# Moving the second gate pass and dealing layer 2 out in even pieces in a Fourier-mixing and gated feed-forward kernel

## Chip, cores, metric

One core of one Trainium2 chip. The time is device microseconds of one execution. The kernel before takes 719.3 us (median of 4 runs, 718.97 to 719.59); repeated runs agree within about 0.15%. One execution of the kernel before was a slow one (1024.69 us at a clock of 0.662); it is left out.

## The reference

```python
def _attn_ref(x):                       # x: 8 x 3008 x 256
    X = np.fft.fft(x, axis=1)
    X = np.fft.fft(X, axis=2)
    return X.real.astype(np.float32)

def _moe_ref(x, w_gate, w_val, w_out):  # 24064 x 256; 256 x 1536, 256 x 1536, 1536 x 256
    g = x @ w_gate
    gelu = 0.5 * g * (1.0 + erf(g * inv_sqrt2))
    val = x @ w_val
    return (gelu * val @ w_out).astype(np.float32)
```

## The kernel before

The real part of a Fourier transform has a symmetry, so each token is worked out together with its mirror token. E and O are the sum and the difference part of a pair. A gate is computed as E + O; then a third matmul adds -2 O into the same PSUM bank (weights M), and the bank holds the mirror token's gate. The gate's bank is therefore read by a GELU twice, the second time after the third matmul.

There are 8 batches; each has three groups of at most 512 token pairs. A group is worked in 12 *blocks* of 128 hidden columns (`fc`); the stretch of the emitted order that belongs to one block is a *slot*. Two blocks of three are *split* (none in the very first group): the value is taken with two matmuls in two banks, and VectorE (three operations) and GpSimd do the rest. The third kind is unsplit: value matmuls E and O, then M later, each followed by one product on VectorE. Layer 2 of a group (96 matmuls) is dealt out over the 12 slots of the next group, and the transform of the next batch is dealt out as *filler*. An *eviction* is an instruction that copies a full PSUM bank to SBUF, and so lets the bank be used again.

All eight PSUM banks are taken: two for gates, three for values, one for layer 2 outputs, two for the transform.

```python
def ps_g():   return psum_pool.tile([128, 512], FP32, tag="g",   bufs=2, name="ps_g")
def ps_v():   return psum_pool.tile([128, 512], FP32, tag="v",   bufs=3, name="ps_v")
def ps_o():   return psum_pool.tile([128, 2, C], FP32, tag="o",  bufs=1, name="ps_o")
def ps_dft(): return psum_pool.tile([128, 512], FP32, tag="dft", bufs=2, name="ps_dft")

def l1_first(ci, fc):
    def run():
        # ... cut: slices, tiles
        pg = ps_g()
        mm(pg, n, "g", "E", fs, E, True, False)
        mm(pg, n, "g", "O", fs, O, False, True)
        gl = gelu_tile()
        nc.scalar.activation(gl[:, 0, :n], pg[:, :n], AF.Gelu)              # L517, first GELU
        pv = ps_v()
        if apart(ci, fc):                                                   # split block
            mm(pv, n, "v", "E", fs, E, True, True)
            po = ps_v()
            mm(po, n, "v", "M", fs, O, True, True)
            # ... ve on VectorE from pv (L524), two halves of vv from po (L528, L530)
        else:
            mm(pv, n, "v", "E", fs, E, True, False)
            mm(pv, n, "v", "O", fs, O, False, True)
            # ... first product on VectorE (L536)
    return run

def l1_second(ci, fc):
    def run():
        # ... cut
        mm(pg, n, "g", "M", fs, O, False, True, skip_group_check=True)      # second gate pass
        if apart(ci, fc):
            # ... second GELU (L550), product on GpSimd (L551)
        else:
            mm(pv, n, "v", "M", fs, O, False, True, skip_group_check=True)
            # ... second GELU (L554), second product on VectorE (L555)
    return run

def l2_unit(ci, sub, sign):       # 12 matmuls of 256 columns into one half of the ps_o bank
    ...

def s1_pack(j0):                  # transform, first stage: 8 matmuls, two evictions on ScalarE (L379)
    def run():
        s1_mm(j0)
        s1_ev(j0, "AA")
    return run

# the loop over the blocks of a group
            for fc in range(NFC):
                first[fc]()
                # ... early work and weight folds of the first batch
                tgt = max(0, len(filler) * (slot + 1 - first_slot) // (nslot - first_slot))
                while fi < tgt:
                    filler[fi]()
                    fi += 1
                if fc > 0:
                    second[fc - 1]()
                tgt = len(pend) * (fc + 1) // NFC
                while done < tgt:             # 8 units on 12 slots: 12 matmuls, or none
                    pend[done]()
                    done += 1
                slot += 1
            second[NFC - 1]()
```

The order in which this code emits instructions is not the order on the engines. A scheduler takes it as a priority and moves instructions when, by its own model, an earlier one would wait.

Of the kernel before, what the change touches and what calls it, by code (L numbers as in the profile page):

```python
# [11 lines left out]
AF = mybir.ActivationFunctionType  # L12
# [6 lines left out]
def _sub(base: bass.AP, free_pattern, free_offset, part_start=0, part_num=None):  # L19
    p_step, p_count = base.ap[0]  # L20
    if part_num is None:
        part_num = p_count - part_start
    pat = [[p_step, part_num]] + [list(x) for x in free_pattern]
    off = base.offset + part_start * p_step + free_offset
    return ap_replace(base, ap=pat, offset=off)
# [10 lines left out]
def kernel(  # L36
# [8 lines left out]
    nc = tc.nc  # L45
# [8 lines left out]
    NFC = F // 128  # L54
# [8 lines left out]
    chunk_off, chunk_len = [], []  # L63
    o = 0
    for gr in groups:
        n = sum(width(k2) for k2 in gr)
# [12 lines left out]
    TOK = max(chunk_len)  # L79
# [5 lines left out]
    G = const_pool.tile([NP, NJ, K2H * 4], BF16)  # L85
# [41 lines left out]
    def ps_v():  # L127
        return psum_pool.tile([128, 512], FP32, tag="v", bufs=3, name="ps_v")
# [362 lines left out]
    def ffn_work(b):  # L491
        l1, l2 = [], []
        cstate = {}




        def apart(ci, fc):
            return fc % 3 != 2 and (b, ci) != (0, 0)

        def mm(ps, n, nm, part, fs, src, start, stop, **kw):
            nc.tensor.matmul(ps[:, :n], W[nm, part][:, fs], src, start=start, stop=stop, **kw)  # L502

        def l1_first(ci, fc):
            def run():
                n = chunk_len[ci]
                c0 = chunk_off[ci]
                E, O = (EO_bufs[b][:, i, c0 : c0 + n] for i in range(2))
                if ci not in cstate:
                    cstate[ci] = {"h": h_tile(), "ps": {}, "pso": {}}  # L510
                st = cstate[ci]
                fs = slice(fc * 128, (fc + 1) * 128)
                pg = ps_g()
                mm(pg, n, "g", "E", fs, E, True, False)
                mm(pg, n, "g", "O", fs, O, False, True)
                gl = gelu_tile()
                nc.scalar.activation(gl[:, 0, :n], pg[:, :n], AF.Gelu)  # L517
                pv = ps_v()
                if apart(ci, fc):
                    mm(pv, n, "v", "E", fs, E, True, True)  # L520
                    po = ps_v()
                    mm(po, n, "v", "M", fs, O, True, True)
                    ve = ve_tile()
                    nc.vector.scalar_tensor_tensor(  # L524
                        ve[:, :n], EB_bufs[b][:, c0 : c0 + n], w128[:, fc : fc + 1], pv[:, :n],
                        op0=ALU.mult, op1=ALU.add)
                    vv = v_tile()
                    nc.vector.scalar_tensor_tensor(  # L528
                        vv[:, 0, :n], po[:, :n], -0.5, ve[:, :n], op0=ALU.mult, op1=ALU.add)
                    nc.vector.scalar_tensor_tensor(  # L530
                        _sub(vv, [[-1, n]], TOK + n - 1), po[:, :n], 0.5, ve[:, :n], op0=ALU.mult, op1=ALU.add)
                    st["ps"][fc] = (pg, vv, gl)
                else:
                    mm(pv, n, "v", "E", fs, E, True, False)
                    mm(pv, n, "v", "O", fs, O, False, True)
                    nc.vector.tensor_tensor(st["h"][:, fc, 0, :n], gl[:, 0, :n], pv[:, :n], op=ALU.mult)  # L536
                    st["ps"][fc] = (pg, pv, gl)
            return run

        def l1_second(ci, fc):  # L540
            def run():
                n = chunk_len[ci]
                c0 = chunk_off[ci]
                O = EO_bufs[b][:, 1, c0 : c0 + n]
                st = cstate[ci]
                fs = slice(fc * 128, (fc + 1) * 128)
                pg, pv, gl = st["ps"].pop(fc)
                mm(pg, n, "g", "M", fs, O, False, True, skip_group_check=True)
                if apart(ci, fc):
                    nc.scalar.activation(_sub(gl, [[-1, n]], TOK + n - 1), pg[:, :n], AF.Gelu)  # L550
                    nc.gpsimd.tensor_tensor(st["h"][:, fc, :, :n], gl[:, :, :n], pv[:, :, :n], op=ALU.mult)  # L551
                else:
                    mm(pv, n, "v", "M", fs, O, False, True, skip_group_check=True)
                    nc.scalar.activation(gl[:, 1, :n], pg[:, :n], AF.Gelu)  # L554
                    nc.vector.tensor_tensor(  # L555
                        _sub(st["h"], [[-1, n]], (fc * 2 + 1) * TOK + n - 1),
                        gl[:, 1, :n], pv[:, :n], op=ALU.mult)
            return run

        def last(ci):  # L560
            return b == B - 1 and ci == len(groups) - 1

        def l2_unit(ci, sub, sign):
            def run():
                st = cstate[ci]
                n = chunk_len[ci]
                m = min(128, n - sub * 128)
                h0 = n - sub * 128 - m if sign else sub * 128
                if sign == 0:
                    st["pso"][sub] = ps_o()  # L570
                pso = st["pso"][sub]
                for fc in range(NFC):
                    nc.tensor.matmul(  # L573
                        pso[:m, sign, :],
                        st["h"][:, fc, sign, h0 : h0 + m],
                        Wo_sb[:, fc, :],
                        start=(fc == 0),
                        stop=(fc == NFC - 1),
                    )
                if last(ci):  # L580

                    osb = osb_tile()
                    if sign == 0:
                        nc.vector.tensor_copy(osb[:m, 0, :], pso[:m, 0, :])  # L584
                        store(b, ci, sub, 0, osb[:, 0, :], nc.sync)
                    else:
                        nc.scalar.activation(osb[:m, 1, :], pso[:m, 1, :], AF.Copy)
                        store(b, ci, sub, 1, osb[:, 1, :], nc.scalar)
                elif sign == 1:
                    osb = osb_tile()  # L590
                    nc.scalar.activation(osb[:m], pso[:m], AF.Copy)  # L591
                    store(b, ci, sub, 0, osb[:, 0, :], nc.sync)
                    store(b, ci, sub, 1, osb[:, 1, :], nc.sync)
            return run

        chunks = []
        for ci in range(len(groups)):
            nsub = (chunk_len[ci] + 127) // 128
            first = [l1_first(ci, fc) for fc in range(NFC)]
            second = [l1_second(ci, fc) for fc in range(NFC)]  # L600

            subs = [nsub - 1, *range(nsub - 1)] if last(ci) else range(nsub)
            l2s = [l2_unit(ci, s, g) for s in subs for g in range(2)]
            chunks.append((first, second, l2s))
        return chunks


    head, s1_mm, s1_ev = dft_work(0)
    NHEAD = 5 + 3
    x_tiles.append(x_tile())  # L610
# [52 lines left out]
    pend = []  # L663
    for b in range(B):
        if b + 1 < B:
            if b > 0:
                x_tiles.append(x_tile())
                load_x(b + 1, [(0, 16), (16, 16)])
            filler = dft_work(b + 1)
        else:  # L670
            filler = []
        chunks = ffn_work(b)
        nslot = len(chunks) * NFC
        first_slot = 0
        if b == 0:

            first_slot = NFC
        slot = 0
        fi = 0
        for first, second, l2s in chunks:  # L680
            done = 0
            for fc in range(NFC):
                first[fc]()
                if b == 0 and slot < NFC:
                    for _ in range(2):
                        if early:
                            early.pop(0)()
                    for f in folds.get(slot, []):
                        f()
                tgt = max(0, len(filler) * (slot + 1 - first_slot) // (nslot - first_slot))  # L690
                while fi < tgt:
                    filler[fi]()
                    fi += 1
                if fc > 0:
                    second[fc - 1]()
                tgt = len(pend) * (fc + 1) // NFC
                while done < tgt:
                    pend[done]()
                    done += 1
                slot += 1  # L700
            second[NFC - 1]()
            pend = l2s
    for u in pend:
        u()


# [1 line left out]
_INS = ['x', 'moe_w_gate', 'moe_w_val', 'moe_w_out']  # L708
# [26 lines left out]
```

## Time and profile before

In tables and profile lines, PE is TensorE (PEld its weight loads), DVE is VectorE, ACT is ScalarE, POOL is GpSimd, and L517 is line 517 of the kernel.

| | before |
|---|---|
| time | 719.3 us |
| span of the profiled run | 716.7 us |
| PE / DVE / ACT / POOL busy | 96 / 80 / 65 / 58% |
| all matmuls at the closest spacing seen | 661 us |
| excess over that spacing, whole span | 46 us |
| the same between 45 and 660 us, single gaps under 25 ns left out | 20.6 us |

From the page (engine: busy us, share of the span, instructions), and the chain that ended last:

```profile
PE 688.0 (96%) x5274; PEld 460.5 (64%) x5336; DVE 572.3 (80%) x923; ACT 466.9 (65%) x892; POOL 412.2 (58%) x242
...
PE 88%; ACT 5%; DVE 4%; issue 2%; DMA 1%; POOL 0%; ACTq 0%; DVEq 0%
```

PE's busy time is not a measure of how full it is, because each matmul's record holds its latency too, and records overlap. The Trainium skill comes to the same conclusion ("Perfetto Trace Analysis", section "Identifying the Most-Contended Engine": occupancy of the matmul row is not a good measure of the distance from the roofline, because pipelined instructions look smaller in the trace). In this trace a 512-column matmul has a record of 0.38 us, and the next one starts 0.216 us after it. The *starts* matter: between two starts of 512-column matmuls lie 216 ns in the median, of 481-column ones 204, of 256-column ones 109, of 96-column ones 42. All four are columns/2.4 + 2.5 ns to within about 1 ns, the formula that "TensorE: Matmul & The Clock Gate", section "Back-to-back issue gap", gives for isolated matmuls. So I call *excess* what a start-to-start distance has beyond that; a missing matmul record is filled in by its weight load. Excess is what the rest of this document counts, by the kind of matmul that came late, leaving out single gaps under 25 ns (so counted, the whole span has 44.6 us of it).

| before, 45 to 660 us | excess |
|---|---|
| before the first gate pass | 10.3 us |
| before a value pass | 7.0 us |
| before a transform matmul | 2.8 us |
| before a second gate pass | 0.5 us |
| before a layer 2 matmul | 0.0 us |

The view of waits, for the weight loads (line, ended by: us in total, times, longest). "Issue" means that the profile names no releaser. A weight load starts when the matmul before it has started (WgE at 306.55 below, the next load at 306.56), so idle time before a weight load tells that this matmul came late:

```profile
PEld L502 <- issue: 19.2, 85, 0.4
...
PEld L573 <- issue: 9.4, 26, 0.7
```

The timeline at one such place, ScalarE and then PE with one weight load (start us, us, engine, line, out<-in, count):

```profile
304.60 0.59 ACT L517 ACTIVATE gelu_sb<-ps_g 128x512 bf16<-128x512 f32 x1
305.14 0.87 ACT L379 ACTIVATE A_sb<-ps_dft 128x384 bf16<-128x384 f32 x2
305.90 0.60 ACT L554 ACTIVATE gelu_sb<-ps_g 128x512 bf16<-128x512 f32 x1
306.38 0.62 ACT L550 ACTIVATE gelu_sb<-ps_g 128x512 bf16<-128x512 f32 x1
```

```profile
305.11 0.38 PE L502 MATMUL ps_g<-EO_sb,WgM 128*128 128x512 bf16 x1
305.33 0.38 PE L502 MATMUL ps_v<-EO_sb,WvM 128*128 128x512 bf16 x1
305.56 0.38 PE L502 MATMUL ps_v<-EO_sb,WvE 128*128 128x512 bf16 x1
305.77 0.38 PE L502 MATMUL ps_g<-EO_sb,WgM 128*128 128x512 bf16 x1
305.99 0.49 PE L573 MATMUL ps_o<-Wo_sb,h_sb 128*97 128x256 bf16 x3
306.55 0.38 PE L502 MATMUL ps_g<-EO_sb,WgE 128*128 128x512 bf16 x1
306.56 0.10 PEld L502 LDWEIGHTS <-WgO 128*128 128x128 bf16 x1 [0.25 <-issue]
```

Read it so. The second gate pass (WgM) at 305.11 is followed, in the emitted order, by no layer 2 matmul in this slot, so the next gate pass (WgE) would come at once and want its bank. The scheduler has pulled a value pass, the next second gate pass and three layer 2 matmuls ahead. Still, the bank's GELU (L554) starts at 305.90 and ends at 306.50; WgE starts at 306.55. The third layer 2 matmul started at 305.99 + 2 x 0.109 = 306.21, so WgE could have started at 306.32: 0.23 us lost. This is how the late ones look throughout: between 60 and 660 us, all 66 first gate passes that came over 60 ns late, and whose record is there, start 49 to 51 ns after the end of a GELU.

### The profile page before, as it was taken

Reading aid. Unit: us, or ns where it says so; the run is one execution under the profiler, and the core shown is the slowest. Engines: PE = TensorE matmul, PEld = TensorE weight load, DVE = VectorE, ACT = ScalarE, POOL = GpSimd, SP = SyncE. Lnnn points to the kernel's source line nnn. Section 1 sums busy time; section 2 is a strip of 40 time slices with the busy share of each in tenths; the row PEclk is TensorE's granted clock in tenths of the full one; section 3 lists DMA queues with packets and bytes.
Section 4 is the critical chain, followed back from the end, with each engine's and each line's share of the span. In section 5 each row is a group of like instructions: output and inputs, shape, how many; then the busy total and the mean of one; then the engine's idle time right before and its main releaser. Section 6 shows DMA issues by size and latency. Waiting matters only on the chain.

```text
span 716.7 us, 14298 instructions
## 1 busy us (share of the span) xinstructions
PE 688.0 (96%) x5274; PEld 460.5 (64%) x5336; DVE 572.3 (80%) x923; ACT 466.9 (65%) x892; POOL 412.2 (58%) x242
## 2 busy tenths in 40 slices
PE   2899999999999999999999999999999999999995
PEld 2556666666667666666666666666666766666664
DVE  7698888798877888788877888779887788888870
ACT  6688567766676666766677656776668666666650
POOL 8205565655556565666566656555565656576760
PEclk9999999999999999999999999999999999999999
DMA  9951512431115111151212421111111111211122
GB/s 247 205 118 23 124 31 46 86 72 35 41 38 119 42 34 43 33 121 38 45 31 53 105 45 34 43 36 37 35 41 42 30 44 31 45 41 38 42 45 66
DMA packets 36277, 43.43 MB, mean 61 GB/s; under 512 B 6668, under 2 KB 33292, under 8 KB 34700
## 3 DMA queue, kind: packets, MB, share of 16 engines
q1 hardware_dynamic: 32432, 30.47, 17.8%
q0 software_dynamic: 3184, 11.57, 8.8%
q8 instruction: 41, 0.67, 0.4%
q10 hardware_dynamic: 592, 0.49, 0.3%
q14 instruction: 28, 0.23, 0.1%
HBM read 29.43 MB, written 24.64 MB: 75 GB/s over the span
## 4 chain that ended last, share of the span: by engine, by line
PE 88%; ACT 5%; DVE 4%; issue 2%; DMA 1%; POOL 0%; ACTq 0%; DVEq 0%
PE ps_o L573 33%; PE ps_g L502 23%; PE ps_v L502 20%; PE ps_dft L402 6%; PE ps_dft L365 3%; ACT gelu_sb L517 1%; ACT gelu_sb L554 1%; ACT A_sb L379 1%; PE ps_dft L427 1%; PE ps_dft L440 1%; DVE x_sb L236 1%; ACT out_sb L591 1%; DVE EO_sb L456 1%; PE ps_dft L452 1%; DVE h_sb L536 1%
## 5 line engine op out<-in xcount | busy, mean ns | idle before, releaser
L551 POOL TENSOR_TENSOR h_sb<-gelu_sb,v_sb 128x1024 bf16<-128x1024 bf16 (+1 forms) x184 | 387.1, 2105 | 277.2 <-ACT gelu_sb L550 156.8
L573 PE MATMUL ps_o<-Wo_sb,h_sb 128*128 128x256 bf16 (+1 forms) x2304 | 295.5, 272 | 4.0 <-DVE out_sb L584 2.2
L573 PEld LDWEIGHTS <-h_sb 128*128 128x128 bf16 (+1 forms) x2304 | 227.7, 100 | 68.3 <-issue 9.4
L517 ACT ACTIVATE gelu_sb<-ps_g 128x512 bf16<-128x512 f32 (+1 forms) x288 | 169.8, 590 | 123.2 <-PE ps_g L502 115.2
L524 DVE SCALAR_TENSOR_TENSOR ve_sb<-EB_sb,w_97,ps_v 128x512 f32<-128x512 bf16 (+1 forms) x184 | 134.1, 733 | 66.2 <-PE ps_v L502 66.0
L528 DVE SCALAR_TENSOR_TENSOR v_sb<-ps_v,ve_sb 128x512 f32<-128x512 f32 (+1 forms) x184 | 124.4, 676 | 13.9 <-POOL h_sb L551 0.5
L530 DVE SCALAR_TENSOR_TENSOR v_sb<-ps_v,ve_sb 128x512 f32<-128x512 f32 (+1 forms) x184 | 123.3, 670 | 0.0
L550 ACT ACTIVATE gelu_sb<-ps_g 128x512 bf16<-128x512 f32 (+1 forms) x184 | 108.6, 590 | 19.2 <-PE ps_g L502 17.7
L502 PE MATMUL ps_v<-EO_sb,WvE 128*128 128x512 bf16 (+1 forms) x288 | 107.8, 374 | 3.2
L502 PE MATMUL ps_g<-EO_sb,WgE 128*128 128x512 bf16 (+1 forms) x287 | 107.4, 374 | 1.6
L502 PE MATMUL ps_v<-EO_sb,WvM 128*128 128x512 bf16 (+1 forms) x288 | 108.0, 375 | 0.3 <-DVE v_sb L530 0.2
L502 PE MATMUL ps_g<-EO_sb,WgM 128*128 128x512 bf16 (+1 forms) x287 | 107.9, 376 | 0.1
L555 DVE TENSOR_TENSOR h_sb<-gelu_sb,ps_v 128x512 bf16<-128x512 bf16 (+1 forms) x104 | 69.7, 671 | 32.5 <-ACT gelu_sb L554 32.5
L591 ACT ACTIVATE out_sb<-ps_o 128x512 f32<-128x512 f32 x92 | 54.8, 595 | 51.2 <-PE ps_o L573 51.2
L502 PE MATMUL ps_g<-EO_sb,WgO 128*128 128x512 bf16 (+1 forms) x231 | 86.4, 374 | 0.0
L536 DVE TENSOR_TENSOR h_sb<-gelu_sb,ps_v 128x512 bf16<-128x512 bf16 (+1 forms) x104 | 69.9, 673 | 5.2 <-ACT gelu_sb L517 4.0
L554 ACT ACTIVATE gelu_sb<-ps_g 128x512 bf16<-128x512 f32 (+1 forms) x104 | 61.0, 590 | 6.3 <-PE ps_g L502 6.2
L412 DVE CAST Z_sb<-ps_dft 128x512 bf16<-128x512 f32 x88 | 60.1, 684 | 1.3 <-PE ps_dft L402 1.3
L402 PE MATMUL ps_dft<-CS,A_sb 128*128 128x256 bf16 x372 | 60.8, 274 | 0.4 <-DVE EO_sb L456 0.3
L402 PEld LDWEIGHTS <-A_sb 128*128 128x128 bf16 x384 | 37.8, 99 | 28.9 <-issue 1.8
L365 PEld LDWEIGHTS <-x_sb 94*128 94x128 bf16 x512 | 31.9, 102 | 31.3 <-DVE x_sb L236 14.9
L379 ACT ACTIVATE A_sb<-ps_dft 128x384 bf16<-128x384 f32 x115 | 50.9, 496 | 0.3 <-PE ps_dft L365 0.3
(102 smaller groups left out, 433.2 us busy)
## 6 DMA issues: line engine op xcount, KB each, us to landing
out_dram<-out_sb SPq DMA_DIRECT2D x361, 64.0 KB, 2.0
x_sb<-in_x_dram POOLq DMA_DIRECT2D x14, 752.0 KB, 8.1
x_plain<-in_x_dram SPq DMA_DIRECT2D x4, 384.0 KB, 7.6
x_plain<-in_x_dram SPq DMA_DIRECT2D x2, 768.0 KB, 7.6
Wo_sb<-in_moe_w_out_dram POOLq DMA_DIRECT2D x2, 384.0 KB, 5.8
wg_hi<-in_moe_w_gate_dram SPq DMA_DIRECT2D x2, 256.0 KB, 3.8
wv_hi<-in_moe_w_val_dram SPq DMA_DIRECT2D x2, 256.0 KB
wg_lo<-in_moe_w_gate_dram SPq DMA_DIRECT2D x2, 256.0 KB, 4.4
```

Of the source, the lines that this page charges most:

```text
L402: nc.tensor.matmul(ps[:, d * C : (d + 1) * C], A[:, cc, k2 + d, :], CS[:, cc, :], start=(cc == 0), stop=(cc == 1),)
L502: nc.tensor.matmul(ps[:, :n], W[nm, part][:, fs], src, start=start, stop=stop, **kw)
L517: nc.scalar.activation(gl[:, 0, :n], pg[:, :n], AF.Gelu)
L524: nc.vector.scalar_tensor_tensor(ve[:, :n], EB_bufs[b][:, c0 : c0 + n], w128[:, fc : fc + 1], pv[:, :n], op0=ALU.mult, op1=ALU.add)
L528: nc.vector.scalar_tensor_tensor(vv[:, 0, :n], po[:, :n], -0.5, ve[:, :n], op0=ALU.mult, op1=ALU.add)
L530: nc.vector.scalar_tensor_tensor(_sub(vv, [[-1, n]], TOK + n - 1), po[:, :n], 0.5, ve[:, :n], op0=ALU.mult, op1=ALU.add)
L536: nc.vector.tensor_tensor(st["h"][:, fc, 0, :n], gl[:, 0, :n], pv[:, :n], op=ALU.mult)
L550: nc.scalar.activation(_sub(gl, [[-1, n]], TOK + n - 1), pg[:, :n], AF.Gelu)
L551: nc.gpsimd.tensor_tensor(st["h"][:, fc, :, :n], gl[:, :, :n], pv[:, :, :n], op=ALU.mult)
L554: nc.scalar.activation(gl[:, 1, :n], pg[:, :n], AF.Gelu)
L555: nc.vector.tensor_tensor(_sub(st["h"], [[-1, n]], (fc * 2 + 1) * TOK + n - 1), gl[:, 1, :n], pv[:, :n], op=ALU.mult)
L573: nc.tensor.matmul(pso[:m, sign, :], st["h"][:, fc, sign, h0 : h0 + m], Wo_sb[:, fc, :], start=(fc == 0), stop=(fc == NFC - 1),)
```

## The change

Its intent: (1) issue the second gate pass of the preceding block directly behind the gate passes of a block, so that the two GELUs follow each other; (2) deal layer 2 out evenly, 8 matmuls a slot, in pieces of 4, across the bounds of the 12-matmul units. No operation is added or removed.

```diff
-        def l1_first(ci, fc):
+        def l1_gate(ci, fc):          # two gate passes, first GELU
...
+        def l1_value(ci, fc):         # two value passes and what follows on VectorE
...
-        def l1_second(ci, fc):
+        def l1_gate2(ci, fc):         # second gate pass, second GELU
...
+        def l1_value2(ci, fc):        # third value pass or GpSimd product
...
+        L2P = 4
-        def l2_unit(ci, sub, sign):
+        def l2_piece(ci, sub, sign, f0):
...
-                for fc in range(NFC):
+                for fc in range(f0, f0 + L2P):
...
+    SLOT = "GgVvfLL"
...
-            for fc in range(NFC):
-                first[fc]()
-                ... filler ...
-                if fc > 0:
-                    second[fc - 1]()
-                tgt = len(pend) * (fc + 1) // NFC
-                while done < tgt:
-                    pend[done]()
-                    done += 1
+            for fc in range(NFC + 1):
+                for step in SLOT:
+                    if step in "GV" and fc < NFC:
+                        parts[step][fc]()
+                    elif step in "gv" and fc > 0:
+                        parts[step][fc - 1]()
+                    elif step == "L" and done < len(pend) and fc < NFC:
+                        pend[done]()
+                        done += 1
+                    elif step == "f" and fc < NFC:
+                        ... filler, as before ...
```

(Comments and "..." lines are mine.) In the letters of `SLOT`: G gate passes, V value passes of this block; g second gate pass, v third value pass or product of the preceding block; f filler; L four layer 2 matmuls. In these letters the slot before was G V f g v and then three L or none.

More of the change, by code (lines that the diff above doesn't have):

```diff
@@ L517, in run @@
                 nc.scalar.activation(gl[:, 0, :n], pg[:, :n], AF.Gelu)
+                st["ps"][fc] = [pg, gl, None]
+            return run
+        def l1_value(ci, fc):
+            def run():
+                n = chunk_len[ci]
+                c0 = chunk_off[ci]
+                E, O = (EO_bufs[b][:, i, c0 : c0 + n] for i in range(2))
+                st = cstate[ci]
+                fs = slice(fc * 128, (fc + 1) * 128)
+                gl = st["ps"][fc][1]
                 pv = ps_v()
@@ L531, in run @@
                         _sub(vv, [[-1, n]], TOK + n - 1), po[:, :n], 0.5, ve[:, :n], op0=ALU.mult, op1=ALU.add)
-                    st["ps"][fc] = (pg, vv, gl)
+                    st["ps"][fc][2] = vv
                 else:
@@ L536, in run @@
                     nc.vector.tensor_tensor(st["h"][:, fc, 0, :n], gl[:, 0, :n], pv[:, :n], op=ALU.mult)
-                    st["ps"][fc] = (pg, pv, gl)
+                    st["ps"][fc][2] = pv
             return run
-        def l1_second(ci, fc):
+        def l1_gate2(ci, fc):
+            def run():
+                n = chunk_len[ci]
+                c0 = chunk_off[ci]
+                O = EO_bufs[b][:, 1, c0 : c0 + n]
+                fs = slice(fc * 128, (fc + 1) * 128)
+                pg, gl, _ = cstate[ci]["ps"][fc]
+                mm(pg, n, "g", "M", fs, O, False, True, skip_group_check=True)
+                dst = _sub(gl, [[-1, n]], TOK + n - 1) if apart(ci, fc) else gl[:, 1, :n]
+                nc.scalar.activation(dst, pg[:, :n], AF.Gelu)
+            return run
+        def l1_value2(ci, fc):
             def run():
@@ L546, in run @@
                 fs = slice(fc * 128, (fc + 1) * 128)
-                pg, pv, gl = st["ps"].pop(fc)
-                mm(pg, n, "g", "M", fs, O, False, True, skip_group_check=True)
+                _, gl, pv = st["ps"].pop(fc)
                 if apart(ci, fc):
-                    nc.scalar.activation(_sub(gl, [[-1, n]], TOK + n - 1), pg[:, :n], AF.Gelu)
                     nc.gpsimd.tensor_tensor(st["h"][:, fc, :, :n], gl[:, :, :n], pv[:, :, :n], op=ALU.mult)
@@ L553, in run @@
                     mm(pv, n, "v", "M", fs, O, False, True, skip_group_check=True)
-                    nc.scalar.activation(gl[:, 1, :n], pg[:, :n], AF.Gelu)
                     nc.vector.tensor_tensor(
@@ L568, in run @@
                 h0 = n - sub * 128 - m if sign else sub * 128
-                if sign == 0:
+                if (sign, f0) == (0, 0):
                     st["pso"][sub] = ps_o()
                 pso = st["pso"][sub]
-                for fc in range(NFC):
+                for fc in range(f0, f0 + L2P):
                     nc.tensor.matmul(
@@ L579, in run @@
                     )
+                if f0 + L2P < NFC:
+                    return
                 if last(ci):
@@ L598, in ffn_work @@
             nsub = (chunk_len[ci] + 127) // 128
-            first = [l1_first(ci, fc) for fc in range(NFC)]
-            second = [l1_second(ci, fc) for fc in range(NFC)]
+            parts = {k: [f(ci, fc) for fc in range(NFC)] for k, f in (
+                ("G", l1_gate), ("V", l1_value), ("g", l1_gate2), ("v", l1_value2))}
             subs = [nsub - 1, *range(nsub - 1)] if last(ci) else range(nsub)
-            l2s = [l2_unit(ci, s, g) for s in subs for g in range(2)]
-            chunks.append((first, second, l2s))
+            l2s = [l2_piece(ci, s, g, f) for s in subs for g in range(2) for f in range(0, NFC, L2P)]
+            chunks.append((parts, l2s))
         return chunks
+    SLOT = "GgVvfLL"
     head, s1_mm, s1_ev = dft_work(0)
@@ L679 @@
         fi = 0
-        for first, second, l2s in chunks:
+        for parts, l2s in chunks:
             done = 0
-            for fc in range(NFC):
-                first[fc]()
-                if b == 0 and slot < NFC:
-                    for _ in range(2):
-                        if early:
-                            early.pop(0)()
-                    for f in folds.get(slot, []):
-                        f()
-                tgt = max(0, len(filler) * (slot + 1 - first_slot) // (nslot - first_slot))
-                while fi < tgt:
-                    filler[fi]()
-                    fi += 1
-                if fc > 0:
-                    second[fc - 1]()
-                tgt = len(pend) * (fc + 1) // NFC
-                while done < tgt:
-                    pend[done]()
-                    done += 1
-                slot += 1
-            second[NFC - 1]()
+            for fc in range(NFC + 1):
[8 more added lines that the diff above has]
+                    elif step == "f" and fc < NFC:
+                        if b == 0 and slot < NFC:
+                            for _ in range(2):
+                                if early:
+                                    early.pop(0)()
+                            for f in folds.get(slot, []):
+                                f()
+                        tgt = max(0, len(filler) * (slot + 1 - first_slot) // (nslot - first_slot))
+                        while fi < tgt:
+                            filler[fi]()
+                            fi += 1
+                slot += fc < NFC
+            assert done == len(pend)
             pend = l2s
```

## The prediction

> **What bounds the kernel now.** TensorE. The page gives PE 96% busy at clock 0.999, but a matmul's record includes its latency (512 columns: 0.38 us), so I count starts. In the timeline two 512-column matmuls start 0.216 us apart, 256-column ones 0.109 us. The Trainium skill, "TensorE: Matmul & The Clock Gate", section "Back-to-back issue gap", gives N/2.4 + 2.5 ns; the trace agrees to 1 ns. So spaced, all 5336 matmuls (one weight load each; 62 matmul records are missing) need 661 us: layer 1 327, layer 2 252, transforms and weight folds 82. Excess over it is 46 us: about 20 before 45 us (input loads, tables, folds), 5 in the tail, and about 20, at 0.6 us per 20 us, in the steady part. The chain of waits agrees: PE 88%.
>
> Of the excess between 45 and 705 us (26 us), 10 us stand before the first gate pass (WgE: its PSUM bank is still read by the second GELU, ACT line 554 in the waits) and 8 us before value passes (banks still read by VectorE); the rest is the tail's single output bank and narrow transform matmuls.
>
> **What the change does.** It adds or removes no matmul, eviction or DMA, only changes the emitted order (the scheduler's priorities). Before, a slot was: two gate passes, two value passes, filler, second gate pass of the preceding block, perhaps its value pass, then 12 or 0 layer 2 matmuls. In a slot with 0, the next gate pass wants the bank of the second gate pass just issued: matmul end to GELU start about 0.09 us, GELU 0.59 us. The timeline shows the scheduler dodging this by pulling the next value pass or three layer 2 matmuls ahead; 0.1 to 0.25 us of wait is left once per three slots.
>
> After, between the second gate pass and the next gate pass lie 2 value passes (0.43), 8 layer 2 matmuls (0.87) and mean filler (0.28): 1.3 to 1.6 us. The two GELUs run back to back: the second ends near 1.9 us into the slot; the slot is 2.0 us without filler, 2.3 on average. This wait should nearly vanish (10 to 2 us), except after an output eviction (0.60 us on ACT) in a slot without filler. Even slots space value passes 2.3 us apart against 2.1 us of VectorE work for a split block (0.73 + 0.68 + 0.67). That is close: the second value bank of two split blocks in a row stays tight by about 0.1 us, more behind a 0.68 us transform cast. I expect these waits to go from 8 to about 5 us. Weight folds now stand directly ahead of the gate passes that need them: up to 0.5 us lost at the start. The tail is unchanged.
>
> **Time.** 10 us saved on the critical path, minus about 1: 719.5 to 710.5 us. Range 704 to 717. Removing every steady wait would give about 700, so over 2% needs nearly all of it: chance 0.14. Within 2%: 0.84. Slower: 0.02.
>
> **What would show it.** The weight-load idle at line 502 put down to "issue" (19 us, 85 times) falls by half or more; waits of WgE on the second GELU almost vanish; both GELUs stand back to back on ACT; layer 2 stands in runs of 8. Wrong if value banks take over: waits before value passes grow past 8 us, released by VectorE.
>
> **What would make it wrong.** The scheduler may reorder the new order too and leave waits of the same size; VectorE or ACT queues may bunch; pieces of layer 2 may wait for POOL's product (2.1 us) at chunk bounds.

## The result

The changed kernel takes 700.5 us (median of 4 runs, 699.92 to 700.9) against 719.29 us of the kernel before. The ratio is 0.9738 (95% interval 0.9721 to 0.9755). A ratio here is the mean time of one kernel's fast runs over that of the other's of the same rounds, so it is not quite the ratio of the two medians. The change saved 18.8 us; 9 were forecast. The measured time lies 3.5 us below the low end of the range.

Page, after:

```profile
PE 674.4 (97%) x5336; PEld 460.2 (66%) x5336; DVE 574.5 (82%) x923; ACT 452.3 (65%) x892; POOL 411.6 (59%) x242
```

The chain that ended last is cut short in this profile (it covers 1% of the span), so nothing is read from it. Waits of the weight loads, after (L595 is layer 2's line now):

```profile
PEld L595 <- issue: 5.5, 9, 0.7
PEld L502 <- issue: 2.6, 11, 0.3
```

The timeline of one whole slot, ScalarE and then PE:

```profile
121.31 0.60 ACT L517 ACTIVATE gelu_sb<-ps_g 128x512 bf16<-128x512 f32 x1 [0.67 <-PE ps_g L502]
121.80 0.59 ACT L560 ACTIVATE gelu_sb<-ps_g 128x512 bf16<-128x512 f32 x1
122.28 0.88 ACT L379 ACTIVATE A_sb<-ps_dft 128x384 bf16<-128x384 f32 x2
```

```profile
120.61 0.38 PE L502 MATMUL ps_g<-EO_sb,WgE 128*128 128x512 bf16 x1
120.83 0.38 PE L502 MATMUL ps_g<-EO_sb,WgO 128*128 128x512 bf16 x1
121.05 0.38 PE L502 MATMUL ps_g<-EO_sb,WgM 128*128 128x512 bf16 x1
121.26 0.38 PE L502 MATMUL ps_v<-EO_sb,WvE 128*128 128x512 bf16 x1
121.48 0.38 PE L502 MATMUL ps_v<-EO_sb,WvM 128*128 128x512 bf16 x1
121.70 0.51 PE L365 MATMUL ps_dft<-G,x_sb 94*128 94x96 bf16 x8
122.04 1.04 PE L595 MATMUL ps_o<-Wo_sb,h_sb 128*128 128x256 bf16 x8
122.91 0.38 PE L502 MATMUL ps_g<-EO_sb,WgE 128*128 128x512 bf16 x1
```

The second GELU (L560, now one line for both kinds of block) follows the first, the two transform evictions come behind it, and it ends at 122.39. The next WgE starts at 122.91, exactly when PE gets there (122.04 + 8 x 0.109). There is half a microsecond to spare, and no gap anywhere in the slot.

| excess, 45 to 660 us | before | after |
|---|---|---|
| first gate pass | 10.3 | 0.3 |
| value pass | 7.0 | 0.5 |
| transform | 2.8 | 1.2 |
| second gate pass | 0.5 | 0.5 |
| sum | 20.6 | 2.5 |

So 18.1 of the 18.8 us are the steady waits. The first 45 us have 17.9 us of excess (18.0 before) and the stretch from 660 us to the end 5.4 us (6.1 before).

### The profile page after: what moved, and what is told of

It is laid out like the page before. It is cut to its first block, busy times and chain, and to the rows that moved or that the text cites. A ratio compares the mean times of both kernels' runs of the same rounds, so it can differ in the third digit from the quotient of the medians.

```text
span 698.0 us, 14358 instructions
## 1 busy us (share of the span) xinstructions
PE 674.4 (97%) x5336; PEld 460.2 (66%) x5336; DVE 574.5 (82%) x923; ACT 452.3 (65%) x892; POOL 411.6 (59%) x242
## 5 line engine op out<-in xcount | busy, mean ns | idle before, releaser
L595 PE MATMUL ps_o<-Wo_sb,h_sb 128*128 128x256 bf16 (+1 forms) x2304 | 299.3, 272 | 3.9 <-DVE out_sb L608 2.2
L595 PEld LDWEIGHTS <-h_sb 128*128 128x128 bf16 (+1 forms) x2304 | 220.4, 100 | 43.9 <-issue 5.5
L560 ACT ACTIVATE gelu_sb<-ps_g 128x512 bf16<-128x512 f32 (+1 forms) x288 | 168.5, 585 | 2.8 <-PE ps_g L502 2.8
L541 DVE SCALAR_TENSOR_TENSOR v_sb<-ps_v,ve_sb 128x512 f32<-128x512 f32 (+1 forms) x184 | 123.0, 669 | 0.0
L502 PE MATMUL ps_g<-EO_sb,WgM 128*128 128x512 bf16 (+1 forms) x288 | 108.3, 376 | 0.0
L502 PE MATMUL ps_g<-EO_sb,WgO 128*128 128x512 bf16 (+1 forms) x288 | 108.2, 376 | 0.0
L502 PE MATMUL ps_v<-EO_sb,WvE 128*128 128x512 bf16 (+1 forms) x288 | 108.0, 375 | 0.0
L502 PE MATMUL ps_g<-EO_sb,WgE 128*128 128x512 bf16 (+1 forms) x288 | 108.0, 375 | 0.0
L502 PE MATMUL ps_v<-EO_sb,WvM 128*128 128x512 bf16 (+1 forms) x288 | 96.9, 376 | 0.0
L575 DVE TENSOR_TENSOR h_sb<-gelu_sb,ps_v 128x512 bf16<-128x512 bf16 (+1 forms) x104 | 70.3, 676 | 16.3 <-ACT gelu_sb L560 14.0
L402 PE MATMUL ps_dft<-CS,A_sb 128*128 128x256 bf16 x372 | 56.8, 274 | 0.3 <-DVE EO_sb L456 0.3
L365 PEld LDWEIGHTS <-x_sb 94*128 94x128 bf16 x512 | 30.5, 102 | 28.9 <-DVE x_sb L236 14.9
L502 PEld LDWEIGHTS <-WvE 128*128 128x128 bf16 x288 | 28.2, 98 | 32.2
```

The costliest lines, as they stand in the source:

```text
L402: nc.tensor.matmul(ps[:, d * C : (d + 1) * C], A[:, cc, k2 + d, :], CS[:, cc, :], start=(cc == 0), stop=(cc == 1),)
L502: nc.tensor.matmul(ps[:, :n], W[nm, part][:, fs], src, start=start, stop=stop, **kw)
L541: nc.vector.scalar_tensor_tensor(_sub(vv, [[-1, n]], TOK + n - 1), po[:, :n], 0.5, ve[:, :n], op0=ALU.mult, op1=ALU.add)
L560: nc.scalar.activation(dst, pg[:, :n], AF.Gelu)
L575: nc.vector.tensor_tensor(_sub(st["h"], [[-1, n]], (fc * 2 + 1) * TOK + n - 1), gl[:, 1, :n], pv[:, :n], op=ALU.mult)
L595: nc.tensor.matmul(pso[:m, sign, :], st["h"][:, fc, sign, h0 : h0 + m], Wo_sb[:, fc, :], start=(fc == 0), stop=(fc == NFC - 1),)
```

## The experiments

Ten more kernels ran, and all gave correct results. All are compared with runs of the kernel before on the same chip and in the same rounds (718.5 to 719.7 us in every set). The theories were: **A/E**, a gate bank is free when its second GELU ends, and the gate pass waits when the PE work between a second gate pass and the next gate pass is shorter than that; **B**, even slots matter because of VectorE's work per value pass; **C**, the place of the second gate pass alone matters; **D**, the early second GELU matters through VectorE's order. E differs from A in counting what stands ahead of the second GELU on ScalarE.

### order_only: part 1 without part 2

```diff
-    SLOT = "GgVvfLL"
+    SLOT = "GgVvfL"
-        L2P = 4
+        L2P = 12
-                    elif step == "L" and done < len(pend) and fc < NFC:
-                        pend[done]()
-                        done += 1
+                    elif step == "L" and fc < NFC:
+                        tgt = len(pend) * (fc + 1) // NFC
+                        while done < tgt:
+                            pend[done]()
+                            done += 1
```

> The new step order, but layer 2 dealt in units of 12 matmuls, 12 or 0 a slot, as before. Theory A (what counts is the PE work between a second gate pass and the next gate pass, which wants its bank; both parts lengthen it): in a slot with 0 layer 2 matmuls only 0.43 us of value passes and 0.28 us of filler stand between them, against about 1.1 us that the GELU needs, so waits stay in a third of the slots: 707 to 713 us, excess between 45 us and the tail 9 to 15 us (22 before, 4 after). Theory B (even spacing of the value passes for VectorE is all): 717 to 720 us. Theory C (the second gate pass's place alone): 700 to 703 us.

Measured: 718.7 us, ratio 0.9995 (0.9978 to 1.0011). No gain at all: A expected 707 to 713, so A's size was missed and C is out; B's 717 to 720 fits so far. The excess before gate passes is even larger than in the kernel before, 14.0 us. It stands where A says: I counted the excess of every kind per slot by the number of layer 2 matmuls in it. The 83 slots with none lost 167 ns each, 13.9 us in all, 13.0 of them before gate passes; the 167 slots with 12 lost 22 ns each, nothing of it before gate passes.

### even_only: part 2 without part 1

```diff
-    SLOT = "GgVvfLL"
+    SLOT = "GVfgvLL"
```

> The old step order (second gate pass after values and filler), layer 2 dealt evenly, 8 a slot. Theory A: 0.87 us of layer 2 stand between second gate pass and next gate pass in every slot, 0.2 us short of what the GELU needs, which the scheduler can mostly dodge: 703 to 709 us. Theory B: 700 to 702 us. Theory C: 717 to 720 us.

Measured: 719.26 us, ratio 1.0002 (0.9987 to 1.0017). No gain either, so B is out, and A, which expected 703 to 709, is at least incomplete. 16.4 us stand before gate passes. The excess of every kind, sorted by the filler in the slot, tells why:

| filler in the slot of even_only | slots | excess per slot |
|---|---|---|
| transform, first stage (evicted by ScalarE) | 55 | 224 ns |
| transform, last stages (mostly evicted by ScalarE) | 62 | 85 ns |
| transform, second stage (evicted by VectorE) | 81 | 29 ns |
| none | 64 | 16 ns |

Of the first row's 12.3 us, 1.4 lie in one slot of the first batch that also holds a weight fold; 10.8 of the 12.3 stand before gate passes (that the expectation of even_dve_evict below gives all 12 us to the gate bank is a little too much). The emitted distance between second gate pass and next gate pass is the same in all rows, 8 layer 2 matmuls (0.87 us), and a third value pass in a third of the slots. It is enough when ScalarE is free. It is not enough when the filler's evictions were emitted ahead of the second GELU. ScalarE and PE in such a slot:

```profile
121.90 0.60 ACT L517 ACTIVATE gelu_sb<-ps_g 128x512 bf16<-128x512 f32 x1 [0.19 <-PE ps_v L502]
122.39 0.87 ACT L379 ACTIVATE A_sb<-ps_dft 128x384 bf16<-128x384 f32 x2
123.13 0.62 ACT L560 ACTIVATE gelu_sb<-ps_g 128x512 bf16<-128x512 f32 x1
```

```profile
122.25 0.38 PE L502 MATMUL ps_g<-EO_sb,WgM 128*128 128x512 bf16 x1
122.48 0.38 PE L502 MATMUL ps_v<-EO_sb,WvM 128*128 128x512 bf16 x1
122.69 1.03 PE L595 MATMUL ps_o<-Wo_sb,h_sb 128*128 128x256 bf16 x8
123.80 0.38 PE L502 MATMUL ps_g<-EO_sb,WgE 128*128 128x512 bf16 x1
```

WgM ended at 122.63, and its GELU started only at 123.13, behind the two evictions. It ended at 123.75; WgE started at 123.80 instead of 123.56. The Trainium skill ("PSUM — Partial Sum Buffer", section "Engine vs sequencer instructions") calls ScalarE's queue strictly first in, first out. The trace agrees: with the usual 0.09 us from matmul end to GELU start, the GELU was ready at 122.72, 0.41 us before it started. This made theory E.

### gate2_after_values: the second gate pass ahead of the filler, but not directly behind the gate passes

```diff
-    SLOT = "GgVvfLL"
+    SLOT = "GVgvfLL"
```

> The kernel after with the second gate pass put behind the two value passes, ahead of the preceding block's value pass, filler and layer 2. Between second gate pass and next gate pass: 0.87 us of layer 2 and 0.28 us of filler, 1.15 us on average. Theory A: just enough, 700 to 704 us. Theory B: 700 to 702 us. Theory C, and a theory D that the early second GELU counts because it lets the unsplit block's product go ahead on VectorE and frees its value bank: 705 us or more.

Measured: 701.42 us, ratio 0.9755 (0.9741 to 0.977), which the interval does not part from the change's 0.9738. So "directly behind the gate passes" is not what counts. It is enough that the second gate pass comes ahead of the filler. Gate excess 0.7 us. This also speaks against D: here the unsplit block's second product stands behind both halves of the split block's value in 65 of 94 cases, as in the kernel before (64 of 92), and little is lost (value excess 1.3 us, 0.5 in the change).

### after_held: no reordering by the scheduler from the second batch on

```diff
-        for parts, l2s in chunks:
-            ...
+        with (tc.manual_schedule() if b > 0 else nullcontext()):
+            for parts, l2s in chunks:
+                ...
```

> The kernel after with every engine held to the emitted order from the second transform batch on (the scheduler may not reorder). Then the unsplit block's second product stands behind all three VectorE operations of the next split block, instead of between the first and the second of them. If my forecast of tight value banks was right for that order (second value bank short by 0.1 us or more in one slot of three, more behind casts), 8 us or more are lost: 708 to 720 us with waits before value passes of over 8 us. If the emitted order is good by itself and the value banks were never tight: 700 to 703 us.

Measured: 726.49 us, ratio 1.0103 (1.0088 to 1.0118), worse than expected by either reading. Value passes waited 5.1 us, close to what the prediction said of them. But gate passes waited 10.8 us and transform matmuls 9.0. In one place read, a row copy on ScalarE waited 2.37 us for VectorE's copy ahead of it and the GELUs stood behind it; 1.58 us of PE went there. So the emitted order alone is not a good order; the scheduler adds to it.

### gap_080 and gap_036: less PE work between second gate pass and next gate pass

```diff
-    SLOT = "GgVvfLL"
+    SLOT = "GVLgvfL"      # gap_080
+    SLOT = "GVLLgvf"      # gap_036
```

> Layer 2 even, second gate pass ahead of the filler on the ScalarE queue, but only 4 of the 8 layer 2 matmuls between it and the next gate pass: 0.44 us of layer 2 and 0.28 us of filler on average (0.44 in slots without filler). The bank needs about 0.9 us of other PE work. Theory E (a bank is waited for when its GELU, with whatever stands ahead of it on ScalarE, takes longer than the PE work before the next gate pass): waits return, above all in slots without filler, 0.1 to 0.25 us each: 708 to 720 us. If evenness and the filler's place alone count: 700 to 703 us.

> As gap_080, with all 8 layer 2 matmuls ahead of the second gate pass: 0.28 us of filler and 0.07 us of value pass, on average, before the next gate pass. Theory E: every slot is short, the scheduler dodges what it can and leaves 0.1 to 0.3 us in most slots: 715 to 740 us, and more than gap_080. If distance does not count: 700 to 703 us.

Measured: 726.31 us (ratio 1.0099, 1.0083 to 1.0115), 6 us above the expected range, and 740.64 us (1.0297, 1.0281 to 1.0313), just above it. Layer 2 is even in both and the second gate pass stands ahead of its slot's filler, so what they change is the distance. Excess before gate passes:

| step order | work behind the second gate pass, mean | gate excess | time |
|---|---|---|---|
| GgVvfLL (the change) | 1.6 us | 0.3 us | 700.5 us |
| GVgvfLL | 1.2 us | 0.7 us | 701.4 us |
| GVLgvfL | 0.8 us | 18.5 us | 726.3 us |
| GVLLgvf | 0.4 us | 35.2 us | 740.6 us |

(The second column adds 0.43 us for two value passes, 0.44 for four layer 2 matmuls, 0.28 for mean filler, 0.07 for a third value pass in a third of the slots.) In gap_080 the slots with second-stage filler, 0.88 us of work, lost 5 ns each before gate passes; those with first-stage filler, 0.78 us, lost 44 ns; those without filler, 0.44 us, lost 161 ns. So the need lies near 0.9 us of work behind the second gate pass, and the scheduler dodges part of what is short. The parts of the wait, added up, give an estimate that agrees: 0.38 us for the matmul's record, 0.09 to the GELU's start, 0.59 for the GELU, 0.05 to the gate pass, less 0.216 for the matmul's own place in the stream, makes 0.89 us. Not all of gap_080's loss is this: 4.4 us stand before layer 2 matmuls (none in the change). All 34 late ones start 0.05 us after the end of ScalarE's output eviction, so there the one output bank came free late.

### even_dve_evict: even_only with the ScalarE evictions taken away

```diff
-    SLOT = "GgVvfLL"
+    SLOT = "GVfgvLL"
-                s1_ev(j0, "AA")
+                s1_ev(j0, "VV")        # in s1_pack, batches 1 to 7
```

> even_only with the evictions of the transform's first stage of batches 1 to 7 on VectorE instead of ScalarE, so that they no longer stand ahead of the second GELU. In even_only, slots with that filler waited 0.22 us each for the gate bank (12 us in all), slots with other PE filler of the same length, evicted by VectorE, 0.03 us. Theory E: those 12 us shrink to 2 to 4 us; VectorE gets 58 us more work (80 to 88% busy) and may give some back in value banks: 706 to 713 us. Distance alone (0.87 us short in every slot): 717 to 721 us.

Measured: 709.41 us, ratio 0.9865 (0.985 to 0.9881), as E expected. The slots with first-stage filler went from 12.3 us of excess to 2.6 (1.4 of each is the weight fold's slot), nothing else of the order was touched, and VectorE went from 81 to 87% busy with value excess falling from 2.8 to 1.7 us. The slots with last-stage filler, still evicted mostly by ScalarE, lost 6.1 us (5.3 in even_only).

### after_held_dve: VectorE alone held to the emitted order

```diff
+        with (tc.manual_schedule(engines={mybir.EngineType.DVE}) if b > 0 else nullcontext()):
```

> The kernel after with VectorE alone held to the emitted order. after_held waited 5 us for value banks behind VectorE's last operation of a split block, about what the prediction said, and 23 us elsewhere. If VectorE's order alone makes the value waits: value-pass waits of 3 to 6 us here, 703 to 708 us. If the other engines' held queues made them: under 1.5 us, 700 to 702 us.

Measured: 706.29 us, ratio 0.9819 (0.9802 to 0.9837). Value passes waited 3.8 us and transform matmuls 3.7; gate passes 0.1. That is the forecast of tight value banks, and it holds for the emitted order of VectorE only. 4.4 of its 8.1 us lie in slots with second-stage filler (2.5 of the 3.8 before value passes), whose cast is VectorE's, so the place of the cast may have a part in it. In the change, the scheduler put the unsplit block's second product between the first and the second operation of the next split block in 73 of 94 cases:

```profile
119.17 0.75 DVE L535 SCALAR_TENSOR_TENSOR ve_sb<-EB_sb,w_97,ps_v 128x512 f32<-128x512 bf16 x1 [1.32 <-PE ps_v L502]
119.91 0.69 DVE L575 TENSOR_TENSOR h_sb<-gelu_sb,ps_v 128x512 bf16<-128x512 bf16 x1
120.51 0.68 DVE L539 SCALAR_TENSOR_TENSOR v_sb<-ps_v,ve_sb 128x512 f32<-128x512 f32 x1
121.11 0.68 DVE L541 SCALAR_TENSOR_TENSOR v_sb<-ps_v,ve_sb 128x512 f32<-128x512 f32 x1
```

The same stretch of after_held_dve, with the product behind all three:

```profile
119.96 0.75 DVE L535 SCALAR_TENSOR_TENSOR ve_sb<-EB_sb,w,ps_v 128x512 f32<-128x512 bf16 x1 [1.32 <-PE ps_v L502]
120.84 0.69 DVE L539 SCALAR_TENSOR_TENSOR v_sb<-ps_v,ve_sb 128x512 f32<-128x512 f32 x1
121.45 0.68 DVE L541 SCALAR_TENSOR_TENSOR v_sb<-ps_v,ve_sb 128x512 f32<-128x512 f32 x1
122.05 0.68 DVE L575 TENSOR_TENSOR h_sb<-gelu_sb,ps_v 128x512 bf16<-128x512 bf16 x1
```

In the change, L575 ends at 120.60 and gives its value bank back then. The next split block's second value pass started at 121.48, while L541 still held another bank until 121.79. The product's place cannot be worth all of it: in gate2_after_values it stands behind both halves in 65 of 94 cases too, and value passes waited 1.3 us there, not 3.8. How much each of the scheduler's moves on VectorE is worth was not parted.

### before_g3: a third gate bank in the kernel before, its order untouched

```diff
-        ... tag="g", bufs=2 ...
+        ... tag="g", bufs=3 ...
-        ... tag="dft", bufs=2 ...
+        ... tag="dft", bufs=1 ...
-            tag, n = (("dft", 2), ("g", 2), ("v", 3))[turn[0] % 3]
+            tag, n = (("g", 3), ("v", 3))[turn[0] % 2]
-  _sub(st["ps_b"], [[1, n]], 0, part_num=1)
+  _sub(st["EB"], [[1, n]], chunk_off[gi], part_num=1)
```

> The kernel before, its order untouched, with a third PSUM bank for the gates, taken from the transforms (two banks to one; one row copy reads the same values from SBUF instead, so that one bank is enough). Theory E says that the gate pass waits for a bank: with a third one the 10 us of waits before gate passes (45 to 660 us) fall under 2 us, and value waits fall from 7 us to under 5 because fewer value passes are pulled ahead; waits before transform matmuls rise from 3 us to 10 us or more, so the time itself is open, 708 to 730 us. Rival: the gate pass is late for another reason (its weight load, its place in the queue): waits before it stay at 8 us or more.

Measured: 725.92 us, ratio 1.009 (1.0076 to 1.0104). Excess before gate passes fell from 10.3 to 0.2 us, so it is the bank that they wait for. The waits of the weight loads show where the time went instead:

```profile
PEld L365 <- issue: 16.8, 74, 0.4
...
PEld L502 <- issue: 3.3, 10, 0.8
```

(L365 is a matmul of the transform's first stage; L502 had 19.2 us before.) Transform matmuls now waited 11.3 us, as expected with one bank. Value passes waited 11.8 us, where under 5 were expected: a miss. Perhaps uneven slots also run into the value banks, and in the kernel before the gate waits had stood in front of some of these; that was not tested. No PSUM bank is left over, so this is a test and no remedy.

### tail_banks: the change, and other banks in the tail

In the last group, nothing follows layer 2, and all its eight outputs take the one output bank in turn. The transform's two banks are idle by then.

```diff
+        def ps_tail(k):
+            if k % 3 == 0:
+                return ps_o()
+            return psum_pool.tile([128, 2, C], FP32, tag="dft", bufs=2, name="ps_tail")
...
-                if (sign, f0) == (0, 0):
-                    st["pso"][sub] = ps_o()
-                pso = st["pso"][sub]
+                if last(ci):
+                    if f0 == 0:
+                        k = 2 * subs_of[ci].index(sub) + sign
+                        st["pso"][sub, sign] = ps_tail(k)
+                    pso = st["pso"][sub, sign]
+                else:
+                    ... as before ...
```

> The kernel after; in the last block group alone, each of the 8 layer 2 outputs takes one of three PSUM banks in turn (the output bank and the two transform banks, idle by then) instead of all taking the one output bank. The tail's waits of layer 2 for that bank are 5 us in the kernel after. Theory: they fall under 1 us, 695.5 to 698 us. Rival: the tail is bound by the last eviction and store, so 699.5 to 700.5 us.

Measured: 695.17 us (5 runs, 694.86 to 695.9), ratio 0.9668 (0.9655 to 0.9681) to the kernel before: faster than expected by 0.3 us, and the best of all. In the kernel after, PE in the tail reads

```profile
686.42 1.47 PE L595 MATMUL ps_o<-Wo_sb,h_sb 128*128 128x256 bf16 x12 [0.47 <-ACT out_sb L611]
688.46 1.47 PE L595 MATMUL ps_o<-Wo_sb,h_sb 128*128 128x256 bf16 x12 [0.57 <-DVE out_sb L608]
690.40 1.47 PE L595 MATMUL ps_o<-Wo_sb,h_sb 128*128 128x256 bf16 x12 [0.47 <-ACT out_sb L611]
```

and here

```profile
682.43 1.47 PE L607 MATMUL ps_o<-Wo_sb,h_sb 128*128 128x256 bf16 x12
683.74 2.78 PE L607 MATMUL ps_tail<-Wo_sb,h_sb 128*128 128x256 bf16 x24
686.36 1.47 PE L607 MATMUL ps_o<-Wo_sb,h_sb 128*128 128x256 bf16 x12
```

without a gap. Excess from 660 us to the end fell from 5.4 to 0.3 us.

## Why the prediction was right or wrong

The prediction was wrong: it said 710.5 us, 704 to 717, and gave 0.14 to a gain over 2%; 700.5 us came. Direction and the mechanism of the gate bank were right, the sizes of the sum's terms were not.

- **What bounds the kernel, and how much can be had.** Right. PE's starts, not its busy time, gave 661 us of needed stream and "about 700" for removing every steady wait. The result is that number.
- **First gate pass, "10 to 2 us".** Nearly right: 10.3 to 0.3. even_only, order_only, the gap runs and before_g3 show that it is the gate bank, and that its need is about 0.9 us of PE work behind the second gate pass. The only eviction that the prediction reckoned with on ScalarE was the output's. That the old order put the filler's ahead of the second GELU, and that this alone undoes an even layer 2, it did not see (even_only).
- **Value passes, "from 8 to about 5 us". This is the step that failed.** Measured: 7.0 to 0.5. The prediction laid a split block's VectorE work end to end against the slot, found the second value bank tight by 0.1 us, and left 5 us for it. after_held_dve shows that such waits come with the emitted order of VectorE (3.8 us; 2.7 of it ends 0.05 us after L541, the last operation of a split block), and that the scheduler's own order does away with most of them. Nor were the waits of before of that kind in the main: 4.4 of their 7.0 us end 0.05 us after L524, the *first* operation of a split block, and either part of the change alone brings value waits to 2.9 (order_only) and 2.8 us (even_only), though the gate waits of these two may hide some. The prediction saw the scheduler dodge in the trace of before, but named it for the new order only as a risk. This term is worth 3.5 of the 9.8 us missed.
- **Transform matmuls, taken as fixed.** 2.8 to 1.2 us, 1.6 us. Either part alone already brings them to 1.3 and 1.6 us; why was not tested.
- **Start, "up to 0.5 us lost", and 1 us taken off in the sum.** Nothing was lost: 18.0 to 17.9 us of excess in the first 45 us. So about 1.1 us was missed here.
- **Tail unchanged.** Right of its single-bank waits: they stood in both kernels, and tail_banks took them away. All excess after 660 us went from 6.1 to 5.4 us, 0.7 us; that stretch still holds some steady work.
- Together: the forecast took 8 + 3 as about 10, less 1 at the start, 9 us; 10.0 + 6.5 + 1.6 + 0.1 + 0.7 = 18.9 came, against 18.8 us in the time. (The forecast's 10 and 8 us of waits are of 45 to 705 us, the measured 10.3 and 7.0 of 45 to 660.)

The signs listed in the prediction all came: weight-load idle at line 502 fell from 19.2 to 2.6 us, the GELUs stand back to back, layer 2 stands in runs of 8, and value waits did not grow.

The two parts do nothing alone (0.9995 and 1.0002) and everything together. Each closes one way of being late, and with either left open the excess stays at 20 to 21 us: a slot without layer 2 has too little PE work behind the second gate pass, and a second gate pass behind the filler has its GELU behind the filler's evictions. Why the excess in both cases comes out so near the old 20.6 us (20.2 and 21.1) was not explained; the waits stand in other slots, so I take it for chance.

## What to carry to other kernels

When two buffers alternate, write down for each how long from the last write to its release, including what stands ahead of the releasing instruction on its in-order engine, and set the bound engine's other work in between to be longer than that in *every* round; an average that fits is not enough, and a round with none of the filler work pays each time. Test the parts of an ordering change together as well as alone: two parts that each gain nothing gave 2.6% here. When a scheduler sits between code and engines, do not cost the emitted order by hand as if it ran: hold the order on one engine to see what the scheduler is worth (26 us here on all engines, about 6 on VectorE alone).

## What the Trainium skill lacked or had wrong

- "TensorE: Matmul & The Clock Gate", section "Back-to-back issue gap", gives, in this section alone, for a real stream of weight load and matmul pairs about 131 ns a matmul at 512 columns and 81 ns at 128, and keeps columns/2.4 + 2.5 ns for isolated ones. Here, with a weight load for every matmul, the second formula is the sustained spacing: 216 ns at 512 columns, 109 at 256, 42 at 96 (medians over the trace after 60 us). At 64 columns it is 29 ns.
- The same page, "Part 3", section "The mechanism", under what overlaps, says that a weight load overlaps a running matmul only when the row groups differ (a sentence above it also allows a background weight buffer). Here every matmul of layer 1 and 2 uses all 128 rows, and each 0.10 us load of 128 columns fits under the 0.109 us stream of 256-column matmuls without a gap (start to start).
- No page of it puts together the time from a second accumulating matmul to the release of its bank, though some of the parts stand on its pages. Here it is 0.38 + 0.09 + 0.59 + 0.05 us: matmul record, start of the GELU, GELU of 128x512, start of the next matmul.
